# Attention and two feed-forward layers on one core: values split into two 16-bit parts, and a two-slope activation that carries the sign of 64-bit weights

## The chip, the core and the metric

The kernel runs on one core of a Trainium2 chip. The core has five engines that run side by side, each through its own instructions in a fixed order: TensorE (PE; its weight loads are shown apart as PEld), VectorE (DVE), ScalarE (ACT), GpSimd (POOL), and SyncE (SP), which issues transfers. The metric is the device time of one execution in microseconds (us).

## The reference

Four batches, eight heads, 576 positions, 64 values per head, in 32-bit floats. The output of attention (2304 rows of 512) goes through two feed-forward layers whose weights are 64-bit floats.

```python
scores = scale * np.matmul(q, k.transpose(0, 1, 3, 2))
thresh = np.max(scores, axis=-1, keepdims=True) - tau
scores = np.where(scores >= thresh, scores, -1000000000.0)
attn = np.exp(scores - np.max(scores, axis=-1, keepdims=True))
attn = attn / (np.sum(attn, axis=-1, keepdims=True) + 1e-09)
x = np.matmul(attn, v)            # then heads side by side: 2304 x 512
h = x @ w_in                      # 512 x 2048, layer 1
x = np.square(np.maximum(h, 0.0)) @ w_out
h = x @ w_in2                     # layer 2
out = np.maximum(0.01 * h, h) @ w_out2
```

## The kernel before, in words

**Two halves.** The first half is attention, with part of layer 1 woven in; the second half is the rest of layer 1 and all of layer 2.

Attention goes by 16 pairs of heads (four pairs to a batch) and 9 steps to a pair: 144 steps, 128 query rows each (`step`, from L507). A step has the score product into PSUM tile `s` (L529), the row maximum `nb` on DVE (L539), the exponential `e` on ACT (L540), the threshold `th` on DVE or POOL (L541, L542), one DVE instruction that applies the threshold and sums the row (L544), `t` (the sum plus a constant, L547) and its reciprocal `r` on DVE (L549), and the scaling of `e` by `r` (L553 to L555).

What follows depends on the pair. In the first five pairs (`nav=5`) `e` stays 32-bit: PE turns it (L565, L566), ACT copies the result out of PSUM into `PT`, and PE multiplies it with the values (`av32`, L631). In the other 11 pairs `e` is split into a 16-bit number and a 16-bit rest (tile `P`, L587 or L308/L310), transfers turn both into `PT` (L593), and PE multiplies them with the values (L627). The 32-bit values `VA` are read there in three parts of 16 bits: the two upper ones side by side in `VA` (written by a subtraction), the third in `VB`. There are four such products to a pair, 44 in all: nine matmuls on the two upper parts, 128 output rows each, and then six on `VB`, 64 rows each. Then ACT and DVE add the two halves of the result (`tmp` L639, `xs` L644), and a transfer stores it.

Layer 1 can start on 256 rows (`ffn`, L651) when all heads of these rows are stored. Seven such groups run in the first half, each through 12 of the 16 blocks of the hidden width: `hp` (L675), relu and square (L682, L684), a rounded part `gh` and the rest `gl` = `r` - `gh` (L297/L299 and L308/L310), then `yy` (L701). The second half goes by items of one block and up to 512 rows: `h_unit` (L811, L819 to L823, `gh`, `gl`) and `y_unit` (L857). An item's `y_unit` is issued behind the `h_unit` of the next two items.

A block of weights comes as 64-bit numbers (`w_block`, L329) in two halves, 64 in all. Each is scaled on ACT (L349), put together from its two words by three DVE instructions (L350 shifts, L352 joins, L354 puts the sign back), rounded (`wh`), and the rest is subtracted (`wl`).

**What sets the order.** A planner in the kernel (`Plan.order`) walks through all operations with a cost for each engine that may take it, and writes each engine's list out. `CFG` holds its prices, its due times and the numbers of buffers. When several engines may take an operation, the prices decide, and they differ by stretch of the program. On the chip each engine keeps its list's order and waits where an operand or a buffer isn't ready.

## Time and profile before

| | |
|---|---|
| median of 3 runs | 1093.3 us (1086.04, 1093.3, 1094.08) |
| the profiled execution | 1087.9 us |
| its span, first to last instruction | 1086.1 us |
| PE busy in the span | 1059.4 us (98%) |
| DVE, ACT, POOL busy | 732.8, 509.1, 342.1 us |

The profile is of one execution. Busy time is the union of an engine's records; a matmul's record is longer than the time until the next one starts, so the rate of PE is read from starts, not from lengths. A wait names what ended last before an instruction could begin.

### The profile page before, as it was taken

The page shows a single profiled execution, that of the slowest core. Times are in us where ns is not written, and L with a number is a line of the kernel's source. Part 1 is how long each engine was busy: PE and PEld are TensorE (multiplying, and loading weights), DVE is VectorE, ACT ScalarE, POOL GpSimd, SP SyncE. Part 2 cuts the span into 40 slices and gives each one's busy share as a digit, 9 for nine tenths or more (in the row PEclk, how much of TensorE's full clock was granted, in tenths as well). Part 3 has the DMA queues.
Part 4 walks back from the last instruction along what each step waited for, and adds up shares of the span by engine and source line. Part 5 has one row for each costly group of instructions (what it writes and reads, how often), then busy time and mean ns, then how long its engine had stood idle before and what let it go on. Part 6 is the DMA issues. An engine that isn't in the chain of part 4 may idle for free.

```text
span 1086.1 us, 17711 instructions
## 1 busy us (share of the span) xinstructions
PE 1059.4 (98%) x6343; PEld 886.1 (82%) x6343; DVE 732.8 (67%) x1557; ACT 509.1 (47%) x902; POOL 342.1 (31%) x421
## 2 busy tenths in 40 slices
PE   8988999999999999999999999999999999999998
PEld 4555778888998889989888888888888888888887
DVE  7999898788988898756999975763423433433343
ACT  6899878876776788735343431221211111111121
POOL 5765778889886676410000000000000000000000
PEclk9999999999999999999999999999999999999999
DMA  7444449998888896745644543610100100010010
GB/s 196 122 133 144 137 108 193 181 171 171 169 171 149 172 169 119 142 83 180 227 138 155 181 147 123 225 41 0 70 8 1 39 20 1 1 40 1 1 40 20
DMA packets 186983, 119.16 MB, mean 110 GB/s; under 512 B 146064, under 2 KB 164624, under 8 KB 186896
## 3 DMA queue, kind: packets, MB, share of 16 engines
q1 hardware_dynamic: 186528, 117.82, 44.3%
q8 instruction: 50, 0.82, 0.3%
q10 hardware_dynamic: 368, 0.21, 0.1%
q14 instruction: 37, 0.30, 0.1%
HBM read 70.98 MB, written 17.83 MB: 82 GB/s over the span
## 4 chain that ended last, share of the span: by engine, by line
PE 65%; DVE 1%; ACT 1%; issue 0%; POOL 0%; ACTq 0%; POOLq 0%; DVEq 0%
PE h L811 26%; PE y L857 26%; PE h L675 5%; PE y L701 5%; PE o L627 2%; PE s L529 2%; DVE e L544 0%; DVE nb L539 0%; DVE P L308 0%; ACT e L540 0%; ACT P L554 0%; DVE gl L308 0%; DVE P L587 0%; ACT tmp L639 0%; POOL t L547 0%
## 5 line engine op out<-in xcount | busy, mean ns | idle before, releaser
L823 DVE TENSOR_TENSOR r<-h,r 128x512 f32<-128x512 f32 (+1 forms) x80 | 51.0, 638 | 211.4 <-ACT r L822 211.4
L822 ACT ACTIVATE r<-h 128x512 f32<-128x512 f32 (+1 forms) x80 | 44.5, 557 | 313.1 <-PE h L811 310.6
L310 POOL TENSOR_TENSOR xl<-xr,xh 128x512 fp32r<-128x512 f32 (+1 forms) x11 | 12.7, 1157 | 418.3 <-ACT xh L297 253.5
L544 DVE SCALAR_TENSOR_TENSOR e<-s,th,e 128x576 f32<-128x576 f32 x144 | 116.8, 814 | 31.5 <-ACT e L540 27.4
L529 PE MATMUL s<-KH,Q 128*128 128x288 f32 (+1 forms) x440 | 121.1, 368 | 10.1 <-DVE e L544 6.6
L540 ACT ACTIVATE e<-s,nb 128x576 f32<-128x576 f32 x144 | 106.7, 742 | 38.5 <-DVE nb L539 22.5
L539 DVE TENSOR_REDUCE nb<-s 128x1 f32<-128x576 f32 x144 | 107.8, 750 | 12.4 <-PE s L529 11.3
L529 PEld LDWEIGHTS s<-KH,Q 128*128 128x128 f32 (+1 forms) x440 | 73.6, 183 | 30.6 <-issue 12.3
L308 DVE TENSOR_TENSOR gl<-r,gh 128x512 fp32r<-128x512 f32 (+1 forms) x129 | 85.6, 664 | 8.2
L587 DVE SCALAR_TENSOR_TENSOR P<-e,r,P 128x576 f16<-128x576 f32 x59 | 57.1, 970 | 2.8 <-ACT P L554 1.7
L819 ACT ACTIVATE r<-h 128x512 f32<-128x512 f32 (+1 forms) x32 | 18.2, 573 | 86.4 <-PE h L811 80.1
L627 PE MATMUL o<-PT,VA 128*128 128x320 f16 (+1 forms) x396 | 56.5, 287 | 0.4 <-DVE xs L644 0.4
L529 PE MATMUL s<-KL,Q 128*128 128x288 f32 x200 | 55.8, 294 | 0.0
L299 DVE CAST gh<-r 128x512 fp32r<-128x512 f32 (+1 forms) x103 | 43.8, 425 | 15.9 <-ACT r L684 7.8
L310 POOL TENSOR_TENSOR gl<-r,gh 128x512 fp32r<-128x512 f32 (+1 forms) x25 | 32.7, 1309 | 58.7 <-issue 45.2
L352 DVE SCALAR_TENSOR_TENSOR wraw<-wraw 128x512 int32<-128x512 int32 x64 | 48.9, 765 | 1.7 <-ACT wraw L349 0.6
L349 ACT ACTIVATE wraw<-wraw 128x512 f32<-128x512 f32 x64 | 43.0, 681 | 9.9 <-DMA wraw<-w 9.7
L354 DVE SCALAR_TENSOR_TENSOR wraw<-wraw 128x512 int32<-128x512 int32 x64 | 45.9, 717 | 0.6
L542 POOL TENSOR_SCALAR th<-nb,ca 128x1 f32<-128x1 f32 x75 | 33.3, 444 | 37.0 <-DVE nb L539 29.3
L627 PEld LDWEIGHTS <-VA 128*128 128x128 bf16 x396 | 35.2, 98 | 10.8 <-issue 0.4
L554 ACT ACTIVATE e<-e,r 128x576 f32<-128x576 f32 x51 | 39.4, 776 | 7.5 <-DVE r L549 6.9
L310 POOL TENSOR_TENSOR P<-e,P 128x576 f16<-128x576 f32 x29 | 38.7, 1339 | 8.5 <-ACT P L297 7.6
(616 smaller groups left out, 3044.5 us busy)
## 6 DMA issues: line engine op xcount, KB each, us to landing
wraw<-w SPq DMA_DIRECT2D x64, 512.0 KB, 4.1
wraw<-qT SPq DMA_DIRECT2D x20, 288.0 KB, 4.2
wraw<-kT SPq DMA_DIRECT2D x20, 288.0 KB, 4.4
out<-yo SPq DMA_DIRECT2D x18, 256.0 KB, 2.0
VA<-vv SPq DMA_DIRECT2D x32, 128.0 KB, 2.8
x2d<-yo SPq DMA_DIRECT2D x16, 256.0 KB, 3.3
xr<-x2d SPq DMA_DIRECT2D x4, 1024.0 KB, 5.8
y1d<-ys SPq DMA_DIRECT2D x14, 256.0 KB, 2.8
```

The lines of the kernel that those rows point to most:

```text
L308: alts.append(("V", dve(n), lambda: nc.vector.tensor_tensor(out=o(), in0=a(), in1=b(), op=alu), kind + "*"))
L310: alts.append(("G", pool2(n), lambda: nc.gpsimd.tensor_tensor(out=o(), in0=a(), in1=b(), op=alu), kind))
L529: nc.tensor.matmul(ps.get()[r, g, 0:S2], lhsT=o.Q.get()[:, q], rhs=(kk.get() if o.KL else f32(kk.get()))[:, g_(g)], start=k == 0 or not o. ...
L539: op(("V", 0.75, lambda: nc.vector.tensor_reduce(out=nb.get(), in_=pv(), axis=AX.XY, op=ALU.max, negate=True)), [ps], [nb], i + CFG["pd1"] ...
L540: op(("A", 0.74, lambda: nc.scalar.activation(e.get(), pv(), AF.Exp, bias=nb.get(), scale=1.0)), [ps, nb], [e], i + CFG["pex"], True)
L544: op(("V", 0.82, lambda: nc.vector.scalar_tensor_tensor(out=e.get(), in0=pv(), scalar=th.get(), in1=e.get(), op0=ALU.is_ge, op1=ALU.mult, ...
L587: op(("V", 0.8, lambda: nc.vector.scalar_tensor_tensor(out=lo(), in0=ev(), scalar=r_.get(), in1=hi(), op0=ALU.mult, op1=ALU.subtract), "*" ...
L627: nc.tensor.matmul(ps.get()[r, c_], lhsT=f_(v), rhs=parts16(pt)[:, j, c_], start=(k == 0), stop=k >= len(prods) - 2)
L675: nc.tensor.matmul(ps.get()[:, i], lhsT=a.get()[:, kc * P:(kc + 1) * P], rhs=x.get()[:, kc], start=(i == 0 and q == 0 and kc == 0), stop=( ...
L701: nc.tensor.matmul(yp[m // 2].get()[:, m % 2], lhsT=a.get()[:, c], rhs=x.get()[:, i], start=(f + i == 0 and q == 0 and m % 2 == 0), stop=( ...
L811: nc.tensor.matmul(ps.get()[:, 0:n], lhsT=a.get()[:, kc * P:(kc + 1) * P], rhs=x.get()[:, kc, 0:n], start=(q == 0 and kc == 0), stop=(q == ...
L857: nc.tensor.matmul(o(), lhsT=l, rhs=r, start=(first and q == 0), stop=(last and q == 2))
```

## The change

The values of the 11 later pairs are scaled by a power of two and kept in two parts of type float16 (tile `V16`) in place of three. The scale comes from the largest absolute value: a DVE maximum per partition (`vmax`), a PE product with a matrix of ones that sums these over the partitions (11 of them, into the PSUM tile `o` that the value products also use), three small DVE instructions and `vback`, the factor that undoes the scale. The six matmuls on `VB` are gone; `tmp` and `xs` are scaled by `vback`, an operand per partition, where they had a constant. The split itself moves: VA and VB came from subtractions, nearly all on POOL; the first new part may run on three engines, the second is one DVE instruction (`scalar_tensor_tensor`).

The ACT instruction on the weights is a Prelu with slope 2^32 below zero, whose result carries the sign through the join, and the DVE instruction of L354 is gone (64 times).

Steps go two by two: `sum`, `t` and `r` are 128x2, `t` and the reciprocal run once for two steps, behind the second step's sum, and what scales `e` comes behind that. `th` is a subtraction of two columns. The scaling of Q is done while it is rounded, and its rest is always a DVE instruction. The rounding of weights may run on POOL too, `e` has four buffers in place of three, and all prices and due times are others. The number of transfers is the same.

```diff
-    lead1=1.311, xsg0=[1], lbm=8, ..., eb=3, ...
+    lead1=0.977, xsg0=[1], lbm=8, ..., eb=4, ...
@@ w_block
-                op(("A", 0.677, lambda u=u: nc.scalar.activation(u(), u(), AF.Copy, scale=2.0 ** -112)), [raw], [raw], pr)
-                op(("V", 0.69, lambda ui=ui, yi=yi: nc.vector.scalar_tensor_tensor(
-                    out=yi(), in0=ui(), scalar=-(1 << 31), in1=yi(), op0=ALU.bitwise_and, op1=ALU.bitwise_or), "*"), [raw], [raw], pr)
+                    op(("A", 0.677, lambda u=u: nc.scalar.activation(u(), u(), AF.Prelu, scale=2.0 ** -112, alpha=2.0 ** 32)), [raw], [raw], pr)
+                    op(shift, [raw], [raw], pr)
+                    op(join, [raw], [raw], pr)
-            op(rnd(lambda wh=wh: wh.get(), y, W), [raw], [wh], pr)
+            op(rnd(lambda wh=wh: wh.get(), y, W, engs="AVG"), [raw], [wh], pr)
@@ prep, split
-            op(times(kr.get, 2 * S), [kr], [kr], at(2))
-                op(sub(lambda h=h: qs(h)[D:P], lambda h=h: q3()[D:P, h], lambda h=h: f32(qs(h)[D:P]), S), [qr, Q], [Q], at(3 + h))
+                op(("V", dve(S), lambda h=h: nc.vector.scalar_tensor_tensor(
+                    out=qs(h)[D:P], in0=q3()[D:P, h], scalar=qsc[D:P], in1=f32(qs(h)[D:P]), op0=ALU.mult, op1=ALU.subtract), "*"), [qr, Q], [Q], at(3 + h))
-        op(sub(lambda: va.get()[:, :, :, 1], lambda: va.get()[:, :, :, 0], lambda: up()[:, :, :, 0], nv), [va], [va], at(11))
-        op(sub(lambda: vb.get(), lambda: va.get()[:, :, :, 1], lambda: up()[:, :, :, 1], nv), [va], [vb], at(13))
+        op(("V", dve(nv), lambda: nc.vector.tensor_reduce(out=mx.get(), in_=va.get(), axis=AX.XYZ, op=ALU.max, apply_absolute_value=True)), [va], [mx], at(10))
+        op(("T", 0.25, lambda: nc.tensor.matmul(st.get()[:, 0:1], lhsT=ones, rhs=mx.get(), start=True, stop=True)), [mx, ones_v], [st], at(10))
+        op(("V", dve(nv), lambda: nc.vector.scalar_tensor_tensor(out=v2(), in0=va.get(), scalar=sc.get(), in1=v1(), op0=ALU.mult, op1=ALU.subtract), "*"),
+           [va, sc, v16], [v16], at(13))
@@ step
-        op(("V", 0.158, lambda: nc.vector.reciprocal(out=r_.get(), in_=t_.get())), [t_], [r_], i + CFG["pd2"], True)
+        if k:
+            op(("V", 0.16, lambda: nc.vector.reciprocal(out=r_.get(), in_=t_.get())), [t_], [r_], i + CFG["pd2"], True)
+        return lambda: rest(i, n, h, t, o, ps, e, r_, k)
@@ values
-        prods += [((lo3, up3)[j % 2], slice(0, w), j, low, j) for j in range(MAIN)]
-        prods += [(r, c_, MAIN, low, MAIN) for r, c_ in ((lo3, slice(0, half)), (up3, slice(half, w)))]
-                nc.tensor.matmul(ps.get()[r, c_], lhsT=f_(v), rhs=parts16(pt)[:, j, c_], start=(k == 0), stop=k >= len(prods) - 2)
+                nc.tensor.matmul(ps.get()[:, 0:w], lhsT=o.V16.get()[:, k if k < NH else k - NH, h].rearrange("p a d -> p (a d)"),
+                                 rhs=parts16(pt)[:, k, 0:w], start=(k == 0), stop=(k == NB - 1))
-        op(("A", act(w, True), lambda: nc.scalar.activation(tmp.get()[m, 0:w], ps.get()[l, 0:w], AF.Copy, scale=1.0 / UP)), [ps], [tmp], pr, CFG["xu"])
+        op(("A", act(w, True) + 0.1, lambda: nc.scalar.activation(tmp.get()[m, 0:w], ps.get()[l, 0:w], AF.Copy, scale=back(l)), "x"), [ps] + uv, [tmp], pr, CFG["xu"])
```

Three places in the engines' lists. First PE, at a value product in the second batch. Before, nine weight loads and matmuls on `VA` (one pair of rows stands for nine) are followed by four pairs on `VB` with 320 columns and two with 160:

```order
L701 MATMUL y_1695<-gh,w9ol 128x256
L627 LDWEIGHTS VA
L627 MATMUL o<-PT,VA 128x320
...
L627 LDWEIGHTS VB
L627 MATMUL o<-PT,VB 64x320
...
L627 MATMUL o<-PT,VB 64x160
...
L701 MATMUL y_1687<-gh,w9oh 128x256
```

With the change PE's list has the product with the ones between two score products, and a value product is nine pairs on `V` (the tile `V16`):

```order
L563 MATMUL s<-KL,Q_1726 128x288
L514 MATMUL o<-vmax,ones 128x1
L563 MATMUL s<-KH,Q_1726 128x288
...
L661 LDWEIGHTS V_1720
L661 MATMUL o<-PT,V_1720 128x320
...
L740 MATMUL y_1581<-gh,w10oh 128x256
```

Six rows of matmuls are gone from each value product, and one small matmul per pair of heads is new.

Second DVE, at the first steps of the first batch, where weights (`wraw`) are put together between the steps:

```order
L350 TENSOR_SCALAR wraw<-wraw 128x512
L544 SCALAR_TENSOR_TENSOR e,sum<-s,th,e 128x576
L549 RECIPROCAL r<-t 128x1
L352 SCALAR_TENSOR_TENSOR wraw<-wraw 128x512
L539 TENSOR_REDUCE nb<-s 128x1
L549 RECIPROCAL r<-t 128x1
L539 TENSOR_REDUCE nb<-s 128x1
L544 SCALAR_TENSOR_TENSOR e,sum<-s,th,e 128x576
L354 SCALAR_TENSOR_TENSOR wraw<-wraw 128x512
```

The same place with the change:

```order
L351 TENSOR_SCALAR wraw<-wraw 128x512
L580 SCALAR_TENSOR_TENSOR e,sum<-s,th,e 128x576
L353 SCALAR_TENSOR_TENSOR wraw<-wraw 128x512
L573 TENSOR_REDUCE nb<-s 128x1
L586 RECIPROCAL r<-t 128x2
L351 TENSOR_SCALAR wraw<-wraw 128x512
L573 TENSOR_REDUCE nb<-s 128x1
L580 SCALAR_TENSOR_TENSOR e,sum<-s,th,e 128x576
L575 TENSOR_TENSOR th<-ca,nb 128x1
```

A half of weights takes two DVE instructions where it took three, and two steps share one reciprocal.

Third POOL, at the start of the second half, where POOL's list of before has come to its end but for four rows. With the change it holds the subtractions for weights (`w0il`: block 0 of layer 2) and for items (`gl`):

```order
L310 TENSOR_TENSOR w0il<-wraw,w0ih 128x512
L310 TENSOR_TENSOR gl_7307<-r_7286,gh_7296 128x512
L310 TENSOR_TENSOR gl_7317<-r_7290,gh_7305 128x512
L310 TENSOR_TENSOR gl_7346<-r_7319,gh_7335 128x512
L310 TENSOR_TENSOR w1il<-wraw,w1ih 128x512
L310 TENSOR_TENSOR gl_7371<-r_7332,gh_7355 128x512
L310 TENSOR_TENSOR w0ol<-wraw,w0oh 128x512
```

These subtractions stood on DVE before.

## Rows read from the trace of the kernel before

**Rows 1.** The page: engines over the whole span, and 40 equal slices of it.

```profile
PE 1059.4 (98%) x6343; PEld 886.1 (82%) x6343; DVE 732.8 (67%) x1557; ACT 509.1 (47%) x902; POOL 342.1 (31%) x421
PE   8988999999999999999999999999999999999998
DVE  7999898788988898756999975763423433433343
```

**Rows 2.** Stretches: length, then busy us (records) of engines, clock, DMA share, GB/s.

```profile
core 0: us, PE busy (x) PEld busy (x) DVE busy (x) ACT busy (x) POOL busy (x), PEclk, DMA share, GB/s
10.00:117.00 107.00, 94.63 (x529) 56.93 (x528) 97.57 (x234) 95.97 (x161) 74.20 (x112) 1.00 0.49 140
117.00:160.00 43.00, 42.57 (x291) 34.64 (x291) 38.96 (x84) 34.70 (x59) 29.99 (x29) 1.00 0.47 125
160.00:490.00 330.00, 323.46 (x2639) 291.06 (x2636) 271.45 (x642) 240.29 (x442) 231.37 (x266) 1.00 0.82 156
490.00:525.00 35.00, 34.25 (x282) 33.87 (x282) 26.47 (x50) 15.80 (x27) 0.00 (x0) 1.00 0.63 206
525.00:720.00 195.00, 195.00 (x909) 163.34 (x908) 162.57 (x303) 65.64 (x114) 2.18 (x3) 1.00 0.49 160
```

**Rows 3.** Chain that ended last, a stretch of the second half: start, us, what.

```profile
588.26 2.72 PE h L811 x12
590.98 2.72 PE y L857 x12
```

**Rows 4.** PE in order of time, two value products: start us, us, what (count).

```profile
300.74 1.40 PE L627 MATMUL o<-PT,VA 128*128 128x320 f16 x9
302.07 0.53 PE L627 MATMUL o<-PT,VB 128*64 128x320 f16 x6
302.53 0.39 PE L701 MATMUL y<-gh,w8oh 128*128 128x256 f32 x1
...
315.46 0.47 PE L627 MATMUL o<-PT,VB 128*64 128x256 f16 x6
315.86 0.74 PE L675 MATMUL h<-xh,w1ih 128*128 128x256 f32 x4
```

**Rows 5.** PE in order of time, 32-bit products in the first batch.

```profile
13.67 0.27 PE L566 MATMUL pt<-eye_sb,e 128*128 128x128 f32 x1
13.78 1.14 PE L529 MATMUL s<-KH,Q 128*128 128x288 f32 x4
14.85 1.66 PE L631 MATMUL o<-PT,VA 128*64 128x256 f32 x10
```

**Rows 6.** Waits of ACT from 10 to 117 us: total us, times, longest.

```profile
ACT PT L297 <- PE pt L566: 4.5, 12, 0.9
ACT e L554 <- DVE r L549: 1.6, 3, 1.0
ACT tmp L639 <- PE o L631: 1.6, 3, 0.9
ACT e L540 <- DVE nb L539: 0.9, 3, 0.4
ACT w1oh L297 <- DVE wraw L354: 0.8, 1, 0.8
ACT w4ih L297 <- DVE wraw L354: 0.5, 1, 0.5
```

**Rows 7.** Groups by shape, 10 to 490 us: count, busy us, mean ns, idle before.

```profile
L352 DVE SCALAR_TENSOR_TENSOR wraw<-wraw 128x512 int32<-128x512 int32 x24 | 21.3, 888 | 0.7 <-ACT wraw L349 0.3
L354 DVE SCALAR_TENSOR_TENSOR wraw<-wraw 128x512 int32<-128x512 int32 x24 | 18.2, 760 | 0.1
```

**Rows 8.** The same groups from 525 to 720 us.

```profile
L354 DVE SCALAR_TENSOR_TENSOR wraw<-wraw 128x512 int32<-128x512 int32 x34 | 23.5, 691 | 0.4
L352 DVE SCALAR_TENSOR_TENSOR wraw<-wraw 128x512 int32<-128x512 int32 x34 | 23.5, 690 | 0.9 <-ACT wraw L349 0.3
```

**Rows 9.** Groups by shape in the whole span.

```profile
L549 DVE RECIPROCAL r<-t 128x1 f32<-128x1 f32 x144 | 22.8, 158 | 3.9 <-POOL t L547 1.4
L587 DVE SCALAR_TENSOR_TENSOR P<-e,r,P 128x576 f16<-128x576 f32 x59 | 57.1, 970 | 2.8 <-ACT P L554 1.7 <-POOL P L553 0.9
L539 DVE TENSOR_REDUCE nb<-s 128x1 f32<-128x576 f32 x144 | 107.8, 750 | 12.4 <-PE s L529 11.3
L823 DVE TENSOR_TENSOR r<-h,r 128x512 f32<-128x512 f32 x64 | 44.2, 691 | 186.1 <-ACT r L822 186.1
L310 POOL TENSOR_TENSOR gl<-r,gh 128x512 fp32r<-128x512 f32 x24 | 32.0, 1332 | 13.5 <-ACT gh L297 12.7 <-ACT P L297 0.5
L349 ACT ACTIVATE wraw<-wraw 128x512 f32<-128x512 f32 x64 | 43.0, 681 | 9.9 <-DMA wraw<-w 9.7
L554 ACT ACTIVATE e<-e,r 128x576 f32<-128x576 f32 x51 | 39.4, 776 | 7.5 <-DVE r L549 6.9
L297 ACT CAST gh<-r 128x512 fp32r<-128x512 f32 x49 | 30.3, 619 | 9.1 <-DVE r L820 3.8 <-PE y L857 1.9 <-DVE r L823 1.9
L540 ACT ACT_TABLE_LOAD x1 | 1.3, 1283 | 2.4 <-issue 2.4
```

**Rows 10.** Busy time from the 60th to the 108th row maximum.

```profile
186.00:350.00 164.00, 160.30 (x1307) 143.95 (x1306) 138.31 (x333) 118.59 (x216) 131.56 (x147) 1.00 0.88 170
```

**Rows 11.** Waits of PE in the whole span: total us, times, longest.

```profile
PE pt L565 <- ACT PT L297: 6.7, 9, 1.2
PE s L529 <- DVE e L544: 6.6, 11, 1.2
```

## What is expected

> **What bounds the kernel now.** I read the page first: PE is busy for 98% of the span, and no other engine above 67% [rows 1]. A high busy share says little by itself, since matmul records overlap, so I went to the stretches [rows 2] and, in each, to the engine that never stands. From 525 us to the end PE has no idle time, and the chain of that half is score after score of 12 matmuls in 2.72 us, layer in and layer out, with nothing between [rows 3]: it is PE's own work, the change takes none of it away, and 561 us of the span are fixed. From 117 to 525 us PE is idle for 0.4 + 6.5 + 0.8 = 7.7 us of 408: PE-bound too, since the matmuls of layer 1 fill what attention leaves. Only before 117 us, where no row of layer 1 is ready and PE has attention alone, do others set the pace: PE stands 12.4 of 107 us [rows 2], and the largest item in its list of waits is for ACT's copies out of PSUM [rows 11]. DVE is busy there for 97.6 us and ACT for 96.0. The granted clock is 1.00 throughout. So the time has three parts: an early one by DVE and ACT, a middle one by PE, a late one by PE that stays.
>
> **The change, part by part.**
>
> *The third part of the values goes (middle, PE).* Six matmuls on VB hold PE from 302.07 to 302.53, 0.46 us, at 320 columns, and from 315.46 to 315.86, 0.40 us, at 256 [rows 4]. Of the 44 products half have either width: 22 x 0.86 = 18.9 us. Nothing hides them, as PE is the bound. The nine matmuls on the upper parts stay nine on the new tile, with the same columns: 0.
>
> *A sum over partitions comes (middle, PE).* 11 products in 32 bits with one column; no row shows one. The nearest below is a 128x128 turn in 32 bits, 0.11 us from start to start (13.67 to 13.78), the nearest above a 32-bit score product, whose four records (two products) take 1.07 us, 0.54 each [rows 5]. It has the weight load of both and fewer columns than either; I take 0.25, or +2.7 us, ends 1.2 and 5.9.
>
> *PE stands in front of it.* PE's list is fixed, so when the maximum is late, the score products and layer 1 behind it wait too, and DVE waits for these scores. PE now waits 1.2 us at the longest for DVE [rows 11]. I put this together with the next part.
>
> *DVE's list in the middle.* Between the 60th and the 108th row maximum, 186 to 350 us, DVE is busy for 138.3 of 164 us [rows 10]. The order of the changed list has there, against before: 11 rests of Q (0.69 us at 512 columns where POOL is idle [rows 8], so 0.8 each at 576, 9 us), six maxima over the values and six second parts (some 0.83 each by the 0.75 us of the row maximum over 576, 10 us), 23 instructions on one column (0.16, 3.5 us), three more rests of P (2.5 us); and 25 reciprocals fewer at 0.158 [rows 9], 18 sums t fewer and 31 thresholds of one step less (together 8.5 us), and some seven subtractions fewer that went to POOL or ACT, VB's among them (7 us). That is +10: 148 us. The stretch should shrink by its share of the 18.9 us, 48 of 108 steps, so 8.4, to 155.6, of which 148 is 95%. Where DVE sets the pace before 117 us, its busy share is 97.6 / 107 = 91% [rows 2]; at that share 148 us want 163, 7 us more than there are. Layer 1's matmuls fill some of it. From 0 to 7, I take +3 us, with the late maxima in it.
>
> *Two-input DVE work beside POOL.* L352, the same instruction on the same shape, takes 888 ns from 10 to 490 us, where POOL works, and 690 ns from 525 to 720, where it has 2.2 us of work [rows 2, 7, 8]. [...] I add nothing: POOL's list of the first half is no longer than before, and the 3 us hold it.
>
> *The sign instruction and the shared reciprocal (early, DVE).* Up to the 40th row maximum (about 115 us) the changed list has 14 two-input instructions on weights fewer, at 0.76 [rows 7], 20 reciprocals fewer at 0.158 [rows 9], and three shifts and ten thresholds more (about 2 us): 10.6 + 3.2 - 2 = 12 us off DVE. ACT's list to its 40th exponential has three scalings fewer at 0.776, five roundings fewer at about 0.62, four activations on weights more at 0.681 [rows 9]: 2.7 us off. So ACT becomes the bound. Its named waits there are 10 us: 6.1 for PE's products and 3.8 for DVE [rows 6]. If all stay, the stretch loses 2.7 us; if those for DVE go, 6.5; were DVE still the bound, 12. I take 6.
>
> *Prelu in place of Copy.* No row shows it. The nearest rows of ACT are a rounding of 512 columns, 0.619, below, and a scaling of 576 columns by an operand, 0.776, above [rows 9]; I price it as the copy whose place it takes, 0.681. At either end the 22 of the early part move ACT by about 2 us, inside the range. A change of function tables would cost 1.28 us a time [rows 9], but the changed list has one table load, as before. [...]
>
> *Steps two by two.* The first step of a pair has its `e` scaled only after the second's sum. That delays, and takes no engine's time; the fourth buffer for `e` is the cover, and without it the exponential of the step after next would wait for a scaling. I price it at 0, with a rival below.
>
> *The second half.* The subtractions for items and weights go to POOL, at 1.33 us where DVE takes about 0.69. The cover is the issue order: between an item's `h_unit` and its `y_unit` lie four stretches of 2.72 us [rows 3], 10.9 us, and relu, square, rounding and rest take 0.6 + 0.69 + 0.62 + 1.33 = 3.2 [rows 9]. While weights are loaded, POOL has per item of 5.44 us one `gl`, about one subtraction of weights and one of rows, 4 us. So 0. If the cover went, each microsecond of lateness would count 80 times or so.
>
> **Sum.** -18.9 + 2.7 + 3 - 6 = -19.2 us on the profiled execution's 1087.9, 1068.7. The four times of the kernel before (three runs and the profiled one) have a mean of 1090.3, 2.4 above the profiled; a run of the changed kernel is then at 1071.
>
> **Rivals.**
>
> *More is gained.* DVE decides the early part (-12), the new products cost 0.11 us, and the lighter lists on DVE and ACT take 5 of the 7.7 us at which PE stands in the middle: -18.9 + 1.2 - 12 - 5 = -34.7, so 1056. For it: in the early part ACT often stands because DVE is late. Against: ACT's work hardly falls, and PE's waits there are for ACT [rows 11].
>
> *DVE takes over the middle.* 7 us lost at 186 to 350 us, the new products at 5.9, the early gain only 2.7: -18.9 + 5.9 + 7 - 2.7 = -8.7, so 1082. For it: 95% of a stretch, on an engine that reached 91% where it was the bound. Against: over the steps 41 to 144 DVE's list is about as long as before, and what one stretch lacks the next may give.
>
> *Slower: pairs of steps.* If PE at each of the 52 pairs behind step 40 has to stand for one more DVE instruction, the second step's maximum of 0.75 us, that is +39: 1110. It decides from 0.37 us a pair (no gain left). For it: PE's waits behind 117 us are for DVE's sums. Against: they are 5 us in all, and e's fourth buffer.
>
> *The change brings nothing to PE* would need PE not to be the bound between 160 and 490 us; its 6.5 idle us of 330 exclude that.
>
> **How the numbers follow.** The likeliest case, 0.62, has the range 1062 to 1079. More gained: 0.13. DVE in the middle: 0.20. Pairs: 0.05. The range from 1056 to 1085 leaves out the pairs, a part of the first rival and a little of the second. A measurement of this kernel can tell about 1% from no change, 10.9 us: below 1082.4 is faster. That holds for the likeliest case, the first rival and a third of the second: 0.82; the rest of the second, 0.13, is within 1%; slower 0.05.
>
> **What would show it.** The value products: nine matmuls, and layer 1's next start 1.33 us behind the first at 320 columns. The first matmul of layer 1, which ends the early part, at about 111 us in place of 117, with ACT busier than DVE before it. From 525 - 19 us on, PE without a gap. If PE's waits between 160 and 490 us rise far over 6.5 us, with DVE named, the second or third rival holds; if PE stands for `gl` on POOL in the second half, the cover that I counted on is not there.

## The result, and the profile after

The changed kernel takes **1095.7 us** (median of 20 runs, 1092.9 to 1098.3); the kernel before takes 1088.6 us in the same comparison (20 runs, 1086.0 to 1094.1). The ratio is 1.0057, with a 95% interval from 1.0045 to 1.0069: slower by 0.6%, which counts as no change within 1%. The forecast was 1071, and 1095.7 lies outside its range. The gain is not small, it is gone, and a little more with it.

The page after (busy us, share of the span, instructions; then the span in 40 slices), against [rows 1]:

```profile
span 1094.5 us, 17082 instructions
...
PE 1046.3 (96%) x6101; PEld 884.3 (81%) x6101; DVE 597.7 (55%) x1082; ACT 572.5 (52%) x1024; POOL 576.9 (53%) x618
...
PE   8899998899899989999999999999999999999998
...
DVE  6899779889999999863558742421111111111111
```

PE's busy time fell by 13.1 us, where the forecast had 16.2, and the span still grew by 8.4 us. PE has eights in the slices 7, 8, 11 and 15, where it had nines, and DVE has nines all the way from slice 10 to 16, where it had eights and nines before.

The stretches after (columns as in [rows 2]):

```profile
10.00:117.00 107.00, 96.08 (x534) 57.31 (x534) 96.44 (x209) 93.28 (x159) 73.51 (x102) 1.00 0.55 160
117.00:160.00 43.00, 41.95 (x279) 33.10 (x278) 31.75 (x63) 32.26 (x57) 23.70 (x33) 1.00 0.45 104
160.00:490.00 330.00, 302.90 (x2346) 284.50 (x2347) 299.10 (x594) 228.21 (x421) 219.82 (x270) 0.98 0.80 150
...
535.00:1080.00 545.00, 544.80 (x2523) 455.52 (x2522) 149.42 (x190) 188.05 (x338) 223.64 (x179) 1.00 0.20 68
```

Read the third line. From 160 to 490 us PE stands for 330 - 302.9 = 27.1 us; before it was 6.5. DVE is busy for 299.1 us, 27.6 more than before [rows 2]; the forecast had 10 more, for about half of this stretch. PE's granted clock is 0.98, where it was 1.00. The fourth line is the second half: PE stands for 0.2 us of 545.

By the trace the first matmul of layer 1 starts at 116.2 us (before: 117.3), the first with 512 columns (second half) at 525.9 (before: 518.8). So the early part won 1.1 us, the middle lost 8.2, and behind it 1.3 more went. The middle between these two matmuls, before and then after (columns as above):

```profile
117.31:518.79 401.48, 393.76 (x3155) 353.23 (x3154) 331.19 (x765) 288.10 (x523) 261.36 (x294) 1.00 0.77 157
116.19:525.90 409.71, 380.75 (x2916) 352.70 (x2916) 345.67 (x672) 280.84 (x512) 268.05 (x320) 0.98 0.74 147
```

PE is busy for 13.0 us less and stands 29.0 us in place of 7.7, 21.2 more: together the 8.2 us. I put a part of its busy time down to the lower clock (0.98); `e3_both` below gives its size.

What PE waits for from 160 to 490 us (total, times, longest), after:

```profile
PE s L563 <- DVE e L580: 16.5, 19, 3.1
PE o L661 <- DVE xs L681: 4.7, 5, 1.1
PE o L661 <- DVE vbound L515: 3.6, 3, 1.3
```

All three name DVE; in the whole span of before the first one, the wait for `e`, was 6.6 us [rows 11]. So what did DVE do with 28 more microseconds? Its groups by shape in that stretch (count, busy us, mean ns of one), first before:

```profile
L541 DVE TENSOR_SCALAR th<-nb,ca 128x1 f32<-128x1 f32 x57 | 11.9, 211 | 0.6
L547 DVE TENSOR_SCALAR t<-sum 128x1 f32<-128x1 f32 x60 | 8.8, 148 | 0.9
```

and after:

```profile
L627 DVE SCALAR_TENSOR_TENSOR P<-e,r,P 128x576 f16<-128x576 f32 x63 | 59.0, 946 | 2.6 <-ACT P L594 1.9 <-POOL P L593 0.6
L575 DVE TENSOR_TENSOR th<-ca,nb 128x1 f32<-128x1 f32 x50 | 22.1, 446 | 0.7
L486 DVE SCALAR_TENSOR_TENSOR Q<-wraw,qsc,Q 64x576 fp32r<-64x576 f32 x18 | 20.1, 1119 | 0.6
L584 DVE TENSOR_SCALAR t<-sum 128x2 f32<-128x2 f32 x26 | 14.5, 559 | 0.4
L525 DVE SCALAR_TENSOR_TENSOR V<-VA,vscale,V 128x640 f16<-128x640 f32 x10 | 10.7, 1071 | 0.0
```

Two of the smallest instructions of the kernel, one and two numbers per partition, take 36.6 us; before they took 20.7 for more work. That is 15.9 of the 27.6 us; the new parts of Q and of the values, the third and the fifth of these lines, are the other candidate (theory B below). A mean of 446 ns for one column says that something else is in it. One line's records show the spread (min/median/max ns of DVE's 72):

```profile
L575 DVE TENSOR_TENSOR th<-ca,nb x72: 130/236/1967, 13.9 to 477.1; 128x1 f32<-128x1 f32 x72
```

And the order of time shows what it is, just ahead of PE's longest stop (start, us):

```profile
287.64 1.28 POOL L310 TENSOR_TENSOR P<-e,P 128x576 f16<-128x576 f32 x1
...
287.71 1.22 DVE L575 TENSOR_TENSOR th<-ca,nb 128x1 f32<-128x1 f32 x1
...
288.88 1.39 POOL L310 TENSOR_TENSOR KL<-wraw,KH 128x576 fp32r<-128x576 f32 x1
288.97 1.92 DVE L486 SCALAR_TENSOR_TENSOR Q<-wraw,qsc,Q 64x576 fp32r<-64x576 f32 x1
...
290.92 0.16 DVE L575 TENSOR_TENSOR th<-ca,nb 128x1 f32<-128x1 f32 x1
291.00 0.81 DVE L580 SCALAR_TENSOR_TENSOR e<-s,th,e 128x576 f32<-128x576 f32 x1
...
291.96 0.58 PE L563 MATMUL s<-KH,Q 128*128 128x288 f32 x1 [3.15 <-DVE e L580]
```

POOL begins a subtraction at 287.64 and ends it at 288.92; `th` begins 0.07 us later and ends at 288.93. The same `th` takes 0.16 us at 290.92, where POOL is idle. Over the whole trace, 57 of DVE's 72 `th` begin while a POOL instruction runs, and their mean is 533 ns; the other 15 have 152. Of its 33 `t`, 23 begin so, with 736 ns, the others 162. Of those that begin so, 40 of the 57 `th` end within 20 ns behind a POOL instruction and 20 of the 23 `t` 20 to 30 ns behind one. Before, 61 of 69 `th` and 63 of 76 `t` began under POOL too, at 211 and 148 ns; the others took 210 and 149. So the form of the two instructions changed how they live beside POOL: `th` became a subtraction of two tensors in SBUF, `t` an instruction on two columns.

I read these ends as a wait until the instruction that POOL is running has ended. The trace alone doesn't show that the form decides; the runs below bear it out for both forms.

### The profile page after: what moved, and what is told of

It reads as the page before. It is cut to its first block, busy times and chain, and to the rows that moved or that the text cites. A ratio compares the mean times of both kernels' runs of the same rounds, so it can differ in the third digit from the quotient of the medians.

```text
span 1094.5 us, 17082 instructions
## 1 busy us (share of the span) xinstructions
PE 1046.3 (96%) x6101; PEld 884.3 (81%) x6101; DVE 597.7 (55%) x1082; ACT 572.5 (52%) x1024; POOL 576.9 (53%) x618
## 4 chain that ended last, share of the span: by engine, by line
PE 55%; DVE 15%; issue 15%; POOL 7%; ACT 5%; DMA 3%; POOLq 0%; DVEq 0%; ACTq 0%
PE y L901 19%; PE h L855 19%; PE h L714 5%; PE s L563 4%; DVE e L580 4%; PE y L740 4%; POOL gl L310 4%; DVE nb L573 3%; PE o L661 2%; DMA PT<-P 2%; DVE P L627 2%; PE o L666 1%; ACT e L574 1%; DVE t L584 1%; DVE th L575 1%
## 5 line engine op out<-in xcount | busy, mean ns | idle before, releaser
L310 POOL TENSOR_TENSOR gl<-r,gh 128x512 fp32r<-128x512 f32 (+1 forms) x150 | 190.5, 1270 | 290.2 <-ACT gh L297 280.7
L563 PE MATMUL s<-KH,Q 128*128 128x288 f32 (+1 forms) x440 | 122.5, 372 | 23.3 <-DVE e L580 18.8
L297 ACT CAST gh<-r 128x512 fp32r<-128x512 f32 (+1 forms) x151 | 89.2, 591 | 63.4 <-DVE r L867 50.2
L310 POOL TENSOR_TENSOR xl<-xr,xh 128x512 fp32r<-128x512 f32 (+1 forms) x54 | 71.2, 1326 | 34.1 <-ACT xh L297 31.1
L353 DVE SCALAR_TENSOR_TENSOR wraw<-wraw 128x512 int32<-128x512 int32 x64 | 66.5, 1039 | 15.1 <-ACT wraw L363 12.3
L661 PE MATMUL o<-PT,V 128*128 128x320 f16 (+1 forms) x396 | 57.9, 291 | 8.3 <-DVE xs L681 4.7
L351 DVE TENSOR_SCALAR wraw<-wraw 128x512 int32<-128x512 int32 x64 | 54.9, 859 | 19.5 <-DMA wraw<-w 19.5
L864 DVE SCALAR_TENSOR_TENSOR r<-h,r 128x512 f32<-128x512 f32 (+1 forms) x32 | 20.9, 657 | 62.2 <-ACT r L863 62.2
L575 POOL TENSOR_TENSOR th<-ca,nb 128x1 f32<-128x1 f32 x72 | 25.3, 352 | 51.6 <-DVE nb L573 46.0
L661 PEld LDWEIGHTS <-V 128*128 128x128 f16 x396 | 36.2, 99 | 19.7 <-issue 8.8
L593 POOL TENSOR_SCALAR e<-e,r 128x576 f32<-128x576 f32 x38 | 30.9, 813 | 18.1 <-DVE r L586 17.6
## 6 DMA issues: line engine op xcount, KB each, us to landing
wraw<-qT SPq DMA_DIRECT2D x20, 288.0 KB, 4.1
wraw<-kT SPq DMA_DIRECT2D x20, 288.0 KB, 4.4
```

The lines of the kernel that those rows point to most:

```text
L297: alts.append(("A", act(n, psum), lambda: nc.scalar.copy(o(), i()), kind))
L310: alts.append(("G", pool2(n), lambda: nc.gpsimd.tensor_tensor(out=o(), in0=a(), in1=b(), op=alu), kind))
L351: shift = ("V", 0.42, lambda yi=yi: nc.vector.tensor_scalar(out=yi(), in0=yi(), scalar1=29, scalar2=None, op0=ALU.logical_shift_right), "*")
L353: join = ("V", 0.69, lambda ui=ui, yi=yi: nc.vector.scalar_tensor_tensor(out=yi(), in0=ui(), scalar=3, in1=yi(), op0=ALU.logical_shift_lef ...
L563: nc.tensor.matmul(ps.get()[r, g, 0:S2], lhsT=o.Q.get()[:, q], rhs=(kk.get() if o.KL else f32(kk.get()))[:, g_(g)], start=k == 0 or not o. ...
L661: nc.tensor.matmul(ps.get()[:, 0:w], lhsT=o.V16.get()[:, k if k < NH else k - NH, h].rearrange("p a d -> p (a d)"), rhs=parts16(pt)[:, k, ...
```

## The experiments

**Theory A**: `th` and `t` wait behind POOL, and DVE, being late with `e`, makes PE wait. **B**: DVE's list has become too long by the new parts of Q and of the values. **C**: the pairs of steps make PE stand. Where it isn't said otherwise, an edit keeps every engine's list in the order of its parent. Ratios are to the kernel before on the same chip at the same time, with 95% intervals; 0.01 is 10.9 us.

### The two small instructions

`e1_th`, on the changed kernel: `th` as one column times -1 plus a per-partition scalar, the form of before.

```diff
-        ("V", 0.15, nc.vector.tensor_tensor(out=th, in0=ca, in1=nb, op=subtract))
+        ("V", 0.15, nc.vector.tensor_scalar(out=th, in0=nb, scalar1=-1.0, scalar2=ca, op0=mult, op1=add))
```

> The changed kernel, but the threshold th on DVE is again a TENSOR_SCALAR of one column (nb times -1 plus ca) in place of a subtraction of two columns; every engine's list keeps its order. Theory A (an instruction with two operands in SBUF, or a two-column one, on DVE waits until the instruction that POOL is running ends): in the changed kernel the 72 thresholds on DVE take 0.53 us where POOL is running (57 of them) and 0.15 alone; here they take 0.21 each everywhere, 17 us less on DVE, of which 6 to 14 us reach the end: 1082 to 1090 us. Theory B (DVE's list in the middle is too long by the rests of Q and the second parts of the values): no gain over 2 us, 1093 to 1098. Theory C (steps two by two delay the scores): no gain, 1093 to 1098.

`e2_t`: on DVE, `t` as two instructions of one column.

```diff
-        nc.vector.tensor_scalar(out=t_, in0=sm, ...)
+        for c in range(2): nc.vector.tensor_scalar(out=t_[:, c:c+1], in0=sm[:, c:c+1], ...)
```

> The changed kernel, but t on DVE is two instructions of one column each in place of one of two columns; order kept. Theory A: t takes 0.74 us under a running POOL instruction (23 of 33) and 0.16 alone in the changed kernel; here two times 0.15 everywhere, 10 us less on DVE, of which 3 to 8 us reach the end: 1088 to 1093 us. Theories B and C: DVE has 33 instructions more, so the same or up to 3 us slower: 1094 to 1099.

`e3_both`: both edits.

> Both edits, order kept. Theory A: 27 us less on DVE, the idle time of PE between 160 and 490 us falls from 27 to about 10 us, and the granted clock stays at 1.00 there: 1070 to 1084 us. Theories B and C: 1093 to 1099, with PE's waits as in the changed kernel.

`e4_before_th`: the reverse, on the kernel before.

```diff
-        nc.vector.tensor_scalar(out=th, in0=nb, scalar1=-1.0, scalar2=ca, op0=mult, op1=add)
+        nc.vector.tensor_tensor(out=th, in0=ca, in1=nb, op=subtract)
```

> The kernel before, but th on DVE is a subtraction of two columns of one element each (TENSOR_TENSOR), as the changed kernel has it; nothing else, order kept. Theory A: 61 of its 69 thresholds start while POOL is running; they go from 0.21 to about 0.5 us, some 18 us more on DVE, of which 4 to 12 reach the end: 1093 to 1101 us where the kernel before takes 1088.6. Theories B and C, where the form of th is of no account: 1088.6, plus or minus 2.

Measured: `e1_th` 1088.3 (0.9978, 0.9960 to 0.9996), `e2_t` 1087.7 (0.9975, 0.9951 to 1.0000), `e3_both` **1078.8** (0.9894, 0.9863 to 0.9925), `e4_before_th` 1100.5 (1.0089, 1.0059 to 1.0119). From the changed kernel's 1.0057, one edit is worth 0.8%, the other 0.8%, both 1.6%, or 17.8 us: they add up. (The two do not divide the stretches alike: in `e1_th` the middle is 9.1 us shorter than in the changed kernel, but the first matmul of layer 1 comes 2.8 us later.) The DVE groups and the stretch of `e3_both` from 160 to 490 us:

```profile
L575 DVE TENSOR_SCALAR th<-nb,ca 128x1 f32<-128x1 f32 x49 | 10.0, 209 | 0.7
L584 DVE TENSOR_SCALAR t<-sum 128x1 f32<-128x1 f32 x52 | 6.0, 145 | 0.0
```
```profile
160.00:490.00 330.00, 311.10 (x2460) 293.01 (x2460) 280.39 (x621) 234.42 (x429) 229.31 (x274) 1.00 0.83 160
```

The two take 16.0 us in place of 36.6, although `t` has twice as many instructions; PE stands for 18.9 us in place of 27.1, and its clock is back at 1.00. Between the two matmuls named above, with PE's list the same as in the changed kernel:

```profile
114.17:508.14 393.97, 374.55 (x2916) 347.73 (x2916) 324.44 (x699) 280.77 (x512) 272.52 (x320) 1.00 0.77 153
```

The middle is 15.7 us shorter than in the changed kernel. PE stands 9.5 us less, and the same matmuls keep it busy for 6.2 us less; I put these 6.2 us down to the clock, 1.00 in place of 0.98 (0.98 of 409.7 us, a rounded share, leaves 8). And of the kernel before with the one instruction changed (the wait from 160 to 490 us):

```profile
L541 DVE TENSOR_TENSOR th<-ca,nb x69: 146/640/1383, 17.4 to 471.4; 128x1 f32<-128x1 f32 x69
```
```profile
PE s L529 <- DVE e L544: 10.0, 15, 1.5
```

Its `th` goes from 211 to 662 ns in the middle (37.7 us in place of 11.9), PE's wait for `e` from 5.2 to 10.0 us there, and the kernel loses 9.7 us by the form of one subtraction of one column. Theory A holds in both directions.

`e12_apart`, on `e3_both`: one `t` for two columns again, which lie one apart (elements 0 and 2 of four).

```diff
-        for c in range(2): nc.vector.tensor_scalar(out=t_[:, c:c+1], in0=sm[:, c:c+1], ...)
+        nc.vector.tensor_scalar(out=t_[:, 0:4:2], in0=sm[:, 0:4:2], ...)
```

> As the run with both forms changed (1078.8), but t is one instruction on two columns again, with the two columns one apart (elements 0 and 2 of four) in place of side by side; order of all lists kept. If what waits for POOL is a one-input instruction on neighbouring columns, t takes about 0.15 to 0.16 us here, and the time is 1076 to 1079. If any instruction on more than one column waits, t takes 0.5 to 0.7 us as in the changed kernel, and the time is about 1086 to 1089, as in the run with th alone mended.

Measured: 1089.2 (0.9998, 0.9983 to 1.0014), and

```profile
L584 DVE TENSOR_SCALAR t<-sum 128x2 f32<-128x2 f32 x26 | 13.2, 507 | 0.4
```

So the gap between the columns changes nothing; that there are two does. The reciprocal on the same two columns takes 159 ns here and in the changed kernel, 158 on one column before [rows 9]: it doesn't wait (in the changed kernel 19 of its 72 begin beside POOL, with 158 ns). `t` took 145 ns on one column and 559 and 507 on two; why it waits on two columns, no run shows.

### The parts of the change alone

`e6_before_v16`: the kernel before with the values in two 16-bit parts and nothing else; lists ordered anew by its planner with its own prices.

> The kernel before with only the values' part: two parts of 16 bits, maximum, product with ones, vback; th, t, Q and the weights as before; lists ordered anew with the prices of before. If the middle stays bound by PE, the 18.9 us of the six matmuls go and some 3 us come: 1071 to 1076 us. If DVE, which gets 22 instructions of 0.8 us in the middle, takes it over, part of it is lost: 1078 to 1086, with PE waiting for DVE's sums for over 12 us behind 160 us.

`e5_before_prelu`: the kernel before with the two-slope activation and without the sign instruction; lists ordered anew.

```diff
-        nc.scalar.activation(u, u, AF.Copy, scale=2.0 ** -112)
+        nc.scalar.activation(u, u, AF.Prelu, scale=2.0 ** -112, alpha=2.0 ** 32)
-        nc.vector.scalar_tensor_tensor(out=y, in0=u, scalar=-(1 << 31), in1=y, op0=bitwise_and, op1=bitwise_or)
```

> The kernel before with only the weights' part of the change: Prelu on ACT, no sign instruction on DVE; the planner orders its lists anew with the prices of before. If the early part is bound by ACT, which loses nothing here, the first matmul of layer 1 comes 1 to 4 us earlier than 117 and the whole takes 1083 to 1088 us where the kernel before takes about 1089. If DVE alone bounds it, 14 to 18 instructions of 0.75 us go: 8 to 12 us, 1077 to 1081.

`e9_v16_prelu`: both parts on the kernel before.

> The kernel before with the values in two 16-bit parts (as in the run with that part alone, 1078.9) and also the two-slope activation in place of the copy and the third instruction on weights; th, t and reciprocal one step at a time as before, lists ordered anew. If the two parts add up as my sum has them, about 4 to 6 us are gained on the run with the values alone: 1073 to 1075. If the 44 DVE instructions saved on weights lie beside waits that others end anyway (as alone: 1089.8 against 1090.6), no gain: 1076 to 1081.

Measured: the values alone 1078.9 (0.9912, 0.9890 to 0.9934), the sign alone 1089.8 (1.0001, 0.9983 to 1.0019), both **1076.5** (0.9876, 0.9847 to 0.9905), the lowest time of all runs. The values bring 9.6 us (7.2 to 12.0) where their terms in my sum made 13.2 (the second range, but PE waits 7.3 us for `e` and not over 12); the sign brings nothing alone in this new order, although DVE has 64 instructions less, and its time lies above both ranges that I had. On top of the values it may bring some us; the intervals overlap. With `th` and `t` in the forms of before, a kernel with both headline parts gains 1.2%: neither the 64-bit weights nor the values need cost time.

`e7_no_pairs`: `e3_both` with the steps one by one (own `sum`, `t`, `r`, and the scaling behind each step); lists ordered anew.

> The kernel with both edits (th and t of one column, 1078.8 us), but steps go one by one again: sum, t and r of one column for each step and the scaling behind it at once; lists ordered anew. Theory C (pairs delay the scores and cost time): faster than 1078.8 by 3 us or more. If pairs only save DVE its 72 reciprocals (0.158 us each, 0.07 to 0.16 from start to start) and their sums: 2 to 9 us slower, 1081 to 1088.

`e8_old_sign`: `e3_both` with the copy and the third DVE instruction for all weights; lists ordered anew.

> The kernel with both edits, but all 64 halves of weights go the old way again: scaling by Copy on ACT (or by POOL, where the planner so chooses), and the sign put back by a third DVE instruction; lists ordered anew. If that instruction is worth what DVE loses in the early part (21 of 0.76 us by the 40th step): 8 to 14 us slower than 1078.8, 1087 to 1093. If ACT bounds the early part: 0 to 5 us slower, 1079 to 1084.

Measured: 1088.0 (0.9981, 0.9963 to 1.0000) and 1099.4 (1.0084, 1.0056 to 1.0112), the second above both of its ranges. Steps one by one are not faster, and PE stands as long from 160 to 490 us, 19.1 us against 18.9 in `e3_both`: nothing speaks for theory C. But I would not read the 9 us as the worth of the pairs, nor the 21 as that of the sign instruction. In both, the new order leaves PE a hole near the start of the second half, 4.2 and 5.3 us long, which neither `e3_both` (0.2 us there) nor the kernel before has; of `e7_no_pairs` (the last column is PE's idle time ahead of it):

```profile
533.50 2.06 PE L849 MATMUL h<-xh,w4ih 128*128 128x512 f32 x4 [4.20 <-DVE r L858]
```

I read it so that the prices in `CFG` fit one list of operations, and the planner's order fits no longer when some are taken out; no run tests that.

### The planner's part

`e11_marked`: the changed kernel, `th` and `t` as they are, with the mark `*` that the planner has for DVE work that must not lie beside POOL's. By the trace POOL then has 136 of 144 `th` and 68 of 72 `t`.

> The changed kernel, its th and t as they are, with only the planner's mark for DVE work that waits for POOL put on both: nearly all of them go to POOL (116 of 124 th, 68 of 72 t). Theory A (these small instructions stand behind POOL's): th and t on DVE stretched no more, PE's idle time from 160 to 490 us down from 27 to some 10 to 15, 1078 to 1086, as with the forms changed. Rival (POOL becomes late, since it has no room for them): PE's waits stay, with POOL's th or t named on DVE, 1090 to 1100.

`e10_true_prices`: `e3_both` with DVE's prices set to what they measure (0.21 for `th`, 0.29 for `t`).

> The changed kernel with th and t in forms that do not wait for POOL, as in the run with both (1078.8), but with the planner told what they measure on DVE (0.21 and 0.29 in place of 0.15 and 0.148), so that more of them go to POOL and all lists are ordered anew. If the prices were a loss of their own, beside the waits: 1070 to 1076. If the order of the lists is a lottery of some 10 us here, anything from 1075 to 1090, with PE's idle time in the middle moving in step.

Measured: 1099.8 (1.0089, 1.0058 to 1.0120) and 1084.9 (0.9956, 0.9937 to 0.9974). The mark does take the waits away (DVE's `th` and `t` fall from 36.6 to 4.2 us in the middle, PE's waits for `e` from 18.8 to 12.2 us in the whole span, its idle time from 160 to 490 us from 27.1 to 20.6), and the kernel is slower than with them: my 1078 to 1086 by theory A were wrong for this run. Two losses lie outside the middle: the first matmul of layer 1 is at 122.7 us in place of 116.2, and there is such a hole too, 4.2 us near the start of the second half. The time is in the range of the rival that I had written down, DVE waiting for `th` or `t` from POOL, but of that wait the middle shows only a part:

```profile
L586 DVE RECIPROCAL r<-t 128x2 f32<-128x2 f32 x49 | 7.7, 156 | 3.9 <-POOL t L584 3.4
```

Truer prices, and the new order that they make, cost `e3_both` 6 us. A new order moves this kernel by about as much as the effects under study, and that is why the verdict rests on the runs that keep the order.

### What is left behind `e3_both`

It is 8 us above the forecast, and PE still stands 18.9 us from 160 to 490 us. Two runs shorten DVE's list there, in the same order: `e13_small_max` leaves out four fifths of the values when it looks for their maximum, `e14_small_q` computes 64 of 576 columns of each rest of Q and leaves the others unset.

`e13_small_max`:

```diff
-        nc.vector.tensor_reduce(out=mx, in_=va, axis=XYZ, op=max, apply_absolute_value=True)
+        nc.vector.tensor_reduce(out=mx, in_=va[:, 0:1], axis=XYZ, op=max, apply_absolute_value=True)
```

> The run with both forms changed (1078.8), the order of all lists kept, but the maximum over the values reads 128 of the 640 columns, so the scale is taken from a part of the values only: DVE has 22 times some 0.6 us less, about 13 us, 6 of them from 160 to 490 us, and the product that waits for the maximum comes earlier. If what PE still stands in the middle (18.9 us from 160 to 490 with both forms changed) is the price of the values' maxima on DVE: 1068 to 1074. If that idle time comes from the rest of DVE's list and from its order: 1076 to 1080.

`e14_small_q`:

```diff
-        out=qs(h)[D:P], in0=q3()[D:P, h], scalar=qsc[D:P], in1=f32(qs(h)[D:P])
+        out=qs(h)[D:P, 0:64], in0=q3()[D:P, h, 0:64], scalar=qsc[D:P], in1=f32(qs(h)[D:P, 0:64])
```

> As before, with the values' maximum whole again, but the subtraction for the lower parts of Q runs over 64 of 576 columns, which leaves most of these parts unset: DVE has 24 times some 0.9 us less, about 20 us, most of it in the middle, in two-input instructions that stand behind POOL. If DVE's list as a whole holds PE in the middle, this brings more than the smaller maxima: 1066 to 1072, PE's idle time from 160 to 490 us down from 19 to under 10. If not: 1076 to 1080.

Measured: 1080.3 (0.9905, 0.9871 to 0.9939) and 1078.4 (0.9884, 0.9832 to 0.9937). No gain from either. In the second, DVE is busy for 10 us less from 160 to 490 us, and PE still stands for 17.7:

```profile
160.00:490.00 330.00, 312.30 (x2465) 293.89 (x2464) 270.36 (x624) 235.63 (x433) 223.05 (x274) 0.99 0.84 160
```
```profile
L580 DVE SCALAR_TENSOR_TENSOR e<-s,th,e 128x576 f32<-128x576 f32 x93 | 75.2, 811 | 21.4 <-ACT e L574 20.6
```

DVE's idle time ahead of `e`, for ACT's exponential, grows to 21.4 us (16.4 in `e3_both`): half of what was saved is spent waiting there. So it is not the length of DVE's list, as far as these two parts make it, and theory B falls. The kernel before with the values alone (`e6_before_v16`), without pairs, with the old `th` and `t`, stands nearly as long, 17.1 us:

```profile
160.00:490.00 330.00, 312.92 (x2472) 293.82 (x2472) 284.80 (x688) 248.93 (x445) 225.18 (x275) 1.00 0.84 161
```

With less work for PE the middle is no longer bound by PE alone, whichever way the steps go. I suspect the order in which scores, maxima, exponentials and layer 1 follow each other; I have no run that splits it further, and it stays open.

## Why the prediction was wrong, point by point

**The step that failed** is "DVE's list in the middle", the +3 us of the sum, with the paragraph on "two-input DVE work beside POOL" behind it. In place of the 3 us PE stood 21.2 us more in the middle than before, and its lower clock, as I read `e3_both`, took some 6 more, for which there was no term. 15.7 us of the two are the forms of `th` and `t` (`e3_both`). The list was counted with "18 sums t fewer and 31 thresholds of one step less" as a gain (8.5 us with the reciprocals). I took both at the durations of another form. The trace before held the evidence against it only for large tiles, and there I had it: [rows 7, 8], 888 ns beside POOL, 690 without. But I took the 0.2 us between these means for a matter of such big instructions alone, and added nothing. The wait did not shrink with the waiting instruction: 40 of the 57 `th` begun beside POOL ended within 20 ns behind one of its instructions, the longest behind the second of two. Begun beside POOL, a one-column `th` took 0.38 us more on average (0.53 in place of 0.15), a 576-column rest of Q 0.54 more (1.36 in place of 0.82). Two short lines of the diff, `tensor_tensor` for `tensor_scalar` and `[P, 2]` for `[P, 1]`, were the change that counted, 17.8 us by `e3_both`. In the steps from the 60th to the 108th maximum DVE was busy for 167.3 of 180.8 us (182.4 to 363.2); I had 148 of 155.6. Without the two forms it is 156.3 of 171.7. (The stretch of before holds 22 of the 44 products, 9.5 us of the saving and not 8.4; that changes little.)

With both forms mended PE still stands 19.4 us in the middle, 11.7 more than before, where I had 3: that part of the step stays open. Larger instructions take longer beside POOL as well (the second parts of the values 1.15 us in the changed kernel, 0.88 elsewhere): in `e3_both` the rests of Q take 1.06 us from 160 to 490 us and the second parts of the values 0.90, for which I had 0.8 and 0.83. But `e14_small_q` took 10 us of the rests off DVE and gained nothing.

**The value products** were mis-sized, to the good. The six matmuls on VB are worth what I had, 18.9 us. But the nine others, which I took to stay as they are, 1.33 us at 320 columns, became cheaper: the next start comes 1.12 us behind the first at 320 columns, and 0.91 at 256.

```profile
318.18 1.38 PE L661 MATMUL o<-PT,V 128*128 128x320 f16 x9 [1.05 <-DVE xs L681]
319.30 0.39 PE L740 MATMUL y<-gh,w11oh 128*128 128x256 f32 x1
```

The kernel before has the same number where a score product, and not VB, follows the nine:

```profile
273.86 1.40 PE L627 MATMUL o<-PT,VA 128*128 128x320 f16 x9
274.99 0.40 PE L529 MATMUL s<-KH,Q 128*128 128x288 f32 x1
```

From start to start, without PE's idle time, the nine come to 52.7 us over all 44 products before and to 45.3 in `e3_both`: 7.4 us that I read as fixed. Score products and layer 1 take 4.7 of it back (I have no run for why), so PE's busy time in the middle falls by 19.2 us in `e3_both`, where I had 16.2.

**The products with ones** cost 0.14 us each where PE doesn't stand (312.92 to 313.06), not 0.25; all 11 come to 2.0 us in place of 2.7.

```profile
312.92 0.28 PE L514 MATMUL o<-vmax,ones 128*128 128x1 f32 x2
313.06 0.36 PE L740 MATMUL y<-gh,w10oh 128*128 128x256 f32 x1
```

**The early part** was mis-sized: -6 forecast, -1.1 measured, -3.1 with both forms mended. To the 40th maximum, before (115.3 us) and after (114.9 us):

```profile
0.00:115.30 115.30, 100.11 (x538) 59.56 (x540) 100.20 (x240) 97.86 (x163) 76.21 (x122) 1.00 0.52 148
```
```profile
0.00:114.90 114.90, 100.04 (x540) 58.92 (x542) 97.98 (x214) 94.42 (x158) 75.19 (x111) 1.00 0.58 167
```

ACT lost 3.4 us of work, near my 2.7. DVE lost 2.2, not 12. Of the 10 us between, the trace shows 16 `th` at 449 ns (7.2 us, where before six at 208 took 1.2, and I had 2 us for ten more with three shifts), `t` at 516, and the shifts of the weights at 582 ns in place of 450 (`TENSOR_SCALAR` on 512 columns, one input: in the whole trace 1.06 us where they begin beside POOL, 0.42 elsewhere). The waits of ACT for DVE didn't go, they grew: for the late reciprocal they were 1.6 us [rows 6] and are now

```profile
ACT e L594 <- DVE r L586: 3.5, 5, 1.3
ACT e L574 <- DVE r L586: 2.5, 4, 1.1
```

With both forms mended they are 3.3 us (1.5 and 1.8), and 3.4 with the steps one by one (`e7_no_pairs`): more than half of the growth is the delay by the two forms, and none of it shows as a price of sharing the reciprocal. That ACT's waits hide what DVE gains would fit the sign instruction, which alone brought nothing (`e5_before_prelu`); the new order of that run leaves it unproven.

**Prelu** costs what the copy cost: 677 ns against 681 [rows 9]. Right.

**Steps two by two** at 0: not refuted, since one by one is not faster (`e7_no_pairs`), nor measured cleanly, since the order differs.

**The second half** at 0 was right: `gl` on POOL is in time, PE stands 0.2 us from 535 to 1080 us. DVE's shifts and joins there take longer beside POOL too (1070 and 1183 ns on average from 535 to 720 us; 424 and 690 from 525 to 720 us before, where POOL had 2.2 us of work [rows 2]), and it costs next to nothing, since PE stands only those 0.2 us. The same kind of delay is free in one half and dear in the other.

**The rivals.** My sign for the second and third rival came true (PE's waits far over 6.5 us, DVE named). The second had the right engine, and its mechanism, the length of DVE's list, was not borne out (`e13_small_max`, `e14_small_q`); nor were the pairs (`e7_no_pairs`). A wait that names DVE says who was late, not why; the why was in the mean of a one-column instruction. "The change brings nothing to PE" I had excluded by PE's idle time before, 6.5 of 330 us; that excludes a PE without use for the saving, not an engine that becomes late by it.

## What to carry to other kernels

When a change alters the form of a small instruction (a per-partition scalar becomes a second tensor, one column becomes two), price it by whether it can wait for the neighbour engine, not by its length: here a `th` that took 0.15 us elsewhere took 0.53 on average where it began beside POOL, and a `t` 0.74 in place of 0.16. Read the mean and the maximum of the smallest groups of the engine that is named in the waits; here a mean of 446 ns on one column pointed at the cause. And when a scheduler orders the lists, test a cause with edits that keep the order, since truer prices, by the new order they made, moved this kernel by 6 us.

## What the runs showed of the hardware

That the wait takes instructions on one column was not expected: `th` took 130 to 161 ns alone and up to 1967 ns beside POOL, 40 of 57 ending within 20 ns behind POOL's instruction. The longest, from 407.15 to 409.11 us, stood behind two of POOL's, a 64-partition sum and the `gl` that followed it without a gap:

```profile
406.97 0.87 POOL L679 TENSOR_TENSOR xs<-xs,tmp 64x320 f32<-64x320 f32 x1
407.80 1.28 POOL L310 TENSOR_TENSOR gl<-r,gh 128x512 fp32r<-128x512 f32 x1
...
407.15 1.97 DVE L575 TENSOR_TENSOR th<-ca,nb 128x1 f32<-128x1 f32 x1
```

Nor was it expected that the one-input `t` waits when it has two columns, side by side or apart (559 and 507 ns on average), while a reciprocal on two columns (159 ns) and `t` on one column (145) do not.

PE's clock came as a second loss. Behind the stop of 3.15 us at 288.8 to 292.0 us, 32-bit products of 256 columns start 0.21 us apart, where they started 0.12 apart before it:

```profile
288.06 0.28 PE L740 MATMUL y<-gl,w4oh 128*128 128x256 f32 x1
...
288.18 0.28 PE L740 MATMUL y<-gh,w4ol 128*128 128x256 f32 x1
```
```profile
294.13 0.41 PE L740 MATMUL y<-gh,w5ol 128*128 128x256 f32 x1
294.34 0.41 PE L740 MATMUL y<-gh,w5oh 128*128 128x256 f32 x1
...
290.00:300.00 10.00, 8.04 (x45) 8.07 (x46) 8.96 (x19) 3.80 (x8) 5.90 (x8) 0.66 0.80 178
```

The granted clock was 0.50 from 294 to 295 us, where it was 1.00 from 288.0 to 288.9, and 0.66 over the 10 us from 290. It was 0.87 from 220 to 230 us, behind 2.8 us of idle time from 210 to 220, and 0.83 from 240 to 250, with 1.7 us of idle time in it. In the kernel before it was 1.00 in each of these stretches of 10 us from 200 to 300 us. So I read that the stops cost more than their own length here, some 6 us in all by `e3_both`.
